# Attention scores of two heads in one product, with keys three units ahead, in a fused attention and feed-forward kernel

## The chip, the cores and the metric

The kernel runs on one core of one Trainium2 chip. The metric is device time in microseconds (us), from start to end of one execution; three executions of the kernel before stand below. The engines are TensorE (PE; its weight loads are listed apart as PEld), VectorE (DVE), ScalarE (ACT), GpSimd (POOL) and SyncE (SP), which issues every transfer of this kernel from one queue, in order.

## What is computed

Windowed attention with a few memory keys, then four gated feed-forward experts, then one more feed-forward layer with a leaky activation:

```python
for c in range(nc):                      # 24 chunks of 32 queries
    k_full = np.concatenate([mem_k, k_ctx], axis=2)   # 8 memory keys, 16 left, 32 own, 8 right
    v_full = np.concatenate([mem_v, v_ctx], axis=2)
    scores = scale * np.matmul(q_c, k_full.transpose(0, 1, 3, 2))
    scores = scores - np.max(scores, axis=-1, keepdims=True)
    a = np.exp(scores)
    a = a / (np.sum(a, axis=-1, keepdims=True) + 1e-09)
    out[:, :, c_start:c_end] = np.matmul(a, v_full)
...
for e in range(E):
    h = np.maximum(x @ w1[e], 0.0)
    out += p[:, e:e + 1] * (h @ w2[e])
...
h = x @ w_in
g = np.maximum(h, 0.0) + alpha * np.minimum(h, 0.0)
return g @ w_out
```

The batch is 2, with 8 heads, 768 positions and head size 64; the experts have 1024 hidden columns each, the last layer 2048. All is fp32.

## The kernel before

**Units.** Attention is cut into 12 units of 128 queries, taken in the order `TURN`. `unit(u)` is a generator that yields between its stages:

- scores on PE: `two<-qk`, 64 rows of the trace per unit. Heads stand in pairs, one head of a pair on partitions 0 to 63, the other on 64 to 127. Each product takes 64 partitions, 32 queries and the 64 keys of their window. The four windows of a block and the two heads of a pair use different parts of the array. The result lies in the two PSUM banks of `two`, one for each head of the pairs.
- the row maximum `mx` and the subtraction `pe` on DVE, then the exponential on ACT, in place in `pe`.
- four transposes `t` on PE, copied by ACT to `pt`.
- products with the values on PE: `x<-v,pt`, 32 rows of the trace per unit. Each takes all 128 partitions, both heads at once: the value tile holds zeros where one head's rows meet the other's columns. The first half of a unit's 32 rows reads value tile 2u, the second half tile 2u+1.
- the sums `dn` (ACT), the reciprocal `rd` and the scaling `xs` (DVE), four transposes `xt` (PE), and copies, sums and roundings into `acc`, `xh` and `xl`, from which the first expert's products read.

**Order.** For the first six units, `att_cycle` writes this order on PE: scores of unit m, value products of unit m-1, a few products on zeros (`keep_warm`, tile `keep`), transposes `t` of unit m and `xt` of unit m-1. From unit 6 on, products of the first expert (`a`, `b`, `d`, `c`) stand between the stages. Instructions issued through `Pinned` stay behind what was traced before them on their engine; the others (`nc.vector`, `nc.gpsimd`) are placed by the scheduler.

**Loads.** `load_qk(u)` brings queries and keys of one unit, 624 KB, in one transfer (unit 0 in two). `qk_all` holds two units. The load of unit u+2 is issued behind the scores of unit u, since it overwrites their keys. `load_v(hu)` brings the values of half a unit in two transfers of 64 partitions, 130 KB each, into one of five tiles `v0` to `v4`. A tile is loaded again when the value products have read it. At the start, DVE and POOL fill these tiles with zeros, and a tile's loads follow its two memsets. At the start SP issues unit 0, unit 1 and five value tiles, in this order.

**After attention.** From about 74 us to the end PE works through the experts and the last layer. Their weights are split on ACT, POOL and DVE; DVE adds the results to `acc`.

Of the kernel before, what the change touches and what calls it, by code (L numbers as in the profile page):

```python
# [10 lines left out]
F32 = mybir.dt.float32  # L11
# [7 lines left out]
B, H, S, D = 2, 8, 768, 64  # L19
CH, LEFT, RIGHT, MEM = 32, 16, 8, 8  # L20
BLK = 128
WIN = CH
NW = BLK // WIN
SHARE = LEFT + RIGHT
KEYS = MEM + LEFT + WIN + RIGHT
STEP = KEYS - SHARE
SPAN = NW * STEP + SHARE
NBLK = S // BLK
NU = B * NBLK
NT, DM = B * S, H * D  # L30
E, F1, F2 = 4, 1024, 2048
P = 128
KD = DM // P
HH = H // 2
HP = HH // 2
VW = 2 * HP * NW * (D + 1)
QW, KW = HP * BLK, HP * SPAN
# [26 lines left out]


@with_exitstack
def tile_kernel(ctx: ExitStack, tc: tile.TileContext, qk, v, wa, wq, dpt, alpha, out):
    nc = tc.nc
    scale = 1.0 / float(D) ** 0.5
    pe_, dve, act, pool, sync = (Pinned(tc, e) for e in (nc.tensor, nc.vector, nc.scalar, nc.gpsimd, nc.sync))  # L70
# [3 lines left out]
    bp = ctx.enter_context(tc.tile_pool(name="bp", bufs=1))  # L74
# [4 lines left out]
    two = scores.enter_context(tc.tile_pool(name="sc", bufs=1, space=bass.MemoryType.PSUM)).tile(  # L79
        [P, 2, 512], F32, tag="two", name="two")  # L80
# [36 lines left out]
    def fill(n):  # L117

        if n > 0:
            wps = alone(f"wps{now[0]}")  # L120
            for _ in range(n):
                pe_.matmul(wps[:, :2 * P].rearrange("p (a n) -> p a n", n=P), warm, warm.unsqueeze(1).to_broadcast([P, 2, P]),
                           start=True, stop=True)
                now[0] += 0.11

    fill(WARM)
    now[0] = 0.0
# [25 lines left out]
    xh = xp.tile([P, 14, NCOL], F32R, name="xh")  # L153
    xl = xp.tile([P, 14, NCOL], F32R, name="xl")

    half = NCOL // 2
    acc = xp.tile([P, KD, 2, 2, half], F32, name="acc")
# [5 lines left out]

    change = [False]
    spare = slice(NCOL // 2, NCOL)
    nc.gpsimd.memset(xh[:, 10:14, spare].bitcast(F32), 0.0)

    def keep_warm(u):

# [73 lines left out]
    def mm(*a, n, took=None, **kw):  # L243
        pe_.matmul(*a, **kw)
        now[0] += took or 0.013 + n / 2.4e3


    qk_all = bp.tile([P, RING, QW + KW], F32, tag="gg", bufs=2, name="qk")
# [3 lines left out]
    for vt in v_t:  # L252
        for e in range(2):
            (pool, dve)[e].memset(vt[:, e], 0.0)
    pt, xs, pe = (bp.tile([P, 2 * HP * BLK], F32, tag="ft", bufs=3, name=x) for x in ("pt", "xs", "pe"))
    pt = pt.rearrange("p (z q) -> p z q", q=BLK)
    xs = xs.rearrange("p (z e d) -> p z e d", e=2, d=D)
# [2 lines left out]
    def v_of(hu):  # L260
        return v_t[hu % RING_V]

    def load_qk(u, half=slice(0, 2)):
        if u >= NU:
            return
        i = 2 * u % RING
        sync.dma_start(qk_all[:, i + half.start:i + half.stop].rearrange("p h x -> p (h x)"),
                       qk[TURN[u], :, half].rearrange("p h x -> p (h x)"))

    v_next = [0]  # L270

    def load_v(hu):
        assert hu == v_next[0]
        v_next[0] += 1
        if hu >= 2 * NU:
            return
        for e in range(2):
            sync.dma_start(v_of(hu)[e::2, e].rearrange("p z w d -> p (z w d)"), v[TURN[hu // 2], e, :, hu % 2])

    def unit(u):  # L280
# [2 lines left out]
        cols = slice(c * BLK, (c + 1) * BLK)  # L283
        win = [slice(w * WIN, (w + 1) * WIN) for w in range(NW)]

        s_ps = two[:, :, :2 * HP * KEYS].rearrange("p e (z k) -> p e z k", k=KEYS)
        now[0] += T_SW
        for half in range(2):
            qk_ = qk_t[(2 * u + half) % RING]
            qv = qk_[:, :QW].rearrange("p (z q) -> p z q", q=BLK)  # L290
            kv = qk_[:, QW:].rearrange("p (z k) -> p z k", k=SPAN)
            for z in range(HP):
                for w in range(NW):
                    for e in range(2):
                        rows = slice(e * D, (e + 1) * D)
                        mm(s_ps[win[w], e, HP * half + z], qv[rows, z, win[w]], kv[rows, z, w * STEP:w * STEP + KEYS],
                           n=KEYS, took=T_S, start=True, stop=True)
        load_qk(u + RING // 2)
        mx = cp.tile([P, 2, 2 * HP], F32, tag="mx", bufs=2, name=f"mx{u}")
        dve.tensor_reduce(out=mx, in_=s_ps, axis=AX.X, op=ALU.max)  # L300
        dve.tensor_tensor(
            out=pe.rearrange("p z k e -> p e z k"), in0=s_ps,
# [17 lines left out]
        for z in range(2 * HP):  # L320
            half, i = divmod(z, HP)
            if z in CUT:
                n = CUT[z]
                parts.append((z, n, bank(f"x{u}_{z}")[:, :2 * n * (D + 1)].rearrange("p (z e d) -> p z e d", e=2, d=D + 1)))
            z0, _, x_ps = parts[-1]
            for w in range(NW):
                mm(x_ps[win[w], z - z0], pt[:, z, win[w]], v_of(2 * u + half)[:, :, i, w], n=2 * (D + 1), took=T_X,
                   start=True, stop=True)
            if i == HP - 1:
                load_v(2 * u + half + RING_V)  # L330
        dn = cp.tile([P, 2 * HP, 2, 1], F32, tag="dn", bufs=2, name=f"dn{u}")
# [48 lines left out]
        if c in MID:  # L380
# [4 lines left out]
            out=xl[:, 10:14, cols], in0=a2, in1=xh[:, 10:14, cols].bitcast(F32), op=sub)  # L385
# [10 lines left out]
    def att_poll(force=False):  # L396

        while True:
            due = [x for x in att["live"] if x[0] <= now[0] and clear(x[2])]
            room = att["next"] < NU and len(att["live"]) < LIVE and clear(att["next"])  # L400
            if due:
                x = due[0]
                try:
                    att["stage"][x[2]] += 1
                    lat = next(x[1])
                    x[0] = now[0] + lat
                except StopIteration:
                    att["live"].remove(x)
                    att["over"].add(x[2])
                    while att["done"] in att["over"]:  # L410
                        att["done"] += 1
            elif room and att["start"] <= now[0]:
                g = unit(att["next"])
                att["start"] = now[0] + (PACE0 if force else PACE)
                att["next"] += 1
                x = [0.0, g, att["next"] - 1]
                att["live"].append(x)
                x[0] = next(g) + now[0]
                att["stage"][x[2]] = 1
            elif force:  # L420
                times = [x[0] for x in att["live"] if clear(x[2])]
                if room:
                    times.append(att["start"])
                now[0] = max(now[0], min(times))
                continue
            else:
                return
# [3 lines left out]
    def att_cycle():  # L431
# [18 lines left out]
        def rest():  # L450
# [4 lines left out]
            begin()  # L455

        x = live[m] = [now[0], unit(m), m]
        att["live"].append(x)
        att["next"] += 1
# [139 lines left out]
    def weights():  # L599
        for p in range(NP):  # L600
            if p != NP1 + 1:
                yield from prep_w1(p)
            if p == NP1:
                yield from prep_w1(p + 1)
            yield from prep_w2(p)
# [61 lines left out]
    def stream(name, gen):  # L667
        streams[name] = [0.0, None, gen]
# [348 lines left out]
        order += [(1, k), (2, k - 1)]  # L1017
    order += [(2, len(tiles) - 1)]

    for i in range(2):  # L1020
        load_qk(0, slice(i, i + 1))
    load_qk(1)
    for hu in range(RING_V):
        load_v(hu)
    stream("w", weights())
    streams["w"][0] = PREP0
    acts = {}
# [26 lines left out]
    for i, (what, k, *other) in enumerate(order):  # L1054
        p, c0, n = tiles[k]
# [42 lines left out]
TURN = (0, 2, 1, 4, 3, 5, 6, 7, 8, 9, 10, 11)  # L1098
# [6 lines left out]
T_S, T_X, T_T, T_SW = 0.021, 0.06, 0.11, 0.1  # L1105
# [20 lines left out]
RING = 4  # L1126
V_ROOM = 1152
RING_V = 5
WARM = 18
PAD = 16  # L1130

# [72 lines left out]
```

## Time and profile before

| | us |
|---|---|
| runs of the kernel before | 808.28, 810.08, 810.2 |
| median | 810.08 |
| the profiled execution's own time | 810.12 |
| its span, first to last instruction | 808.3 |
| PE busy, share of the span | 795.1, 98% |
| DVE, ACT, POOL busy | 576.9, 324.8, 572.9 |
| granted TensorE clock | 1.000 |

The time outside the span (810.12 - 808.3 = 1.8 us) lies around the program. The page gives busy time, slices of the span, transfers, the chain of work that ended last, and groups of instructions. The views asked of the trace beside it are the chain in order of time, the timeline of an engine, and transfers issued in a stretch with their time to landing. Nearly every instruction has line 61, that of the helper `Pinned`, so rows are told apart by tile names. A line `x64` on PE counts rows of the trace: a product in plain fp32 that isn't a transpose shows as two of them, so the 32 score products that the program has for a unit are 64 rows.

### The profile page before, as it was taken

The numbers are of one execution on the slowest core, as the hardware profiler recorded it, in microseconds if no ns is written. First come the engines' busy times: TensorE is split into PE (matmuls) and PEld (weight loads), VectorE is DVE, ScalarE is ACT, GpSimd is POOL, SyncE is SP. The second block draws the span as 40 slices with busy tenths as digits, with TensorE's granted clock in tenths as the row PEclk, the third lists the DMA queues.
The fourth block names the chain that finished last, engine by engine and source line by source line (L and its number), as shares of the span: only waits on it lengthen the run. The fifth ranks groups of instructions, "written<-read, shape, count | busy, mean of one in ns | idle before, by whom it ended". The sixth has DMA issues, their size and how long they took to land.

```text
span 808.3 us, 13680 instructions
## 1 busy us (share of the span) xinstructions
PE 795.1 (98%) x5127; PEld 722.6 (89%) x5127; DVE 576.9 (71%) x1009; ACT 324.8 (40%) x726; POOL 572.9 (71%) x598
## 2 busy tenths in 40 slices
PE   7999999999999999999999999999999999999997
PEld 6779989989989889889899899999898988998996
DVE  4666367777777777777777878589975777676554
ACT  4667524224134133133133233154452664565441
POOL 2686767696796696696696783197764978978621
PEclk9999999999999999999999999999999999999999
DMA  8882111341331341322332312001002122221004
GB/s 250 275 276 78 53 53 40 118 143 40 118 103 42 118 124 60 118 78 66 118 106 79 106 51 89 4 27 50 30 26 92 51 81 89 81 92 66 1 1 156
DMA packets 29730, 71.62 MB, mean 89 GB/s; under 512 B 4448, under 2 KB 10592, under 8 KB 29664
## 3 DMA queue, kind: packets, MB, share of 16 engines
q1 hardware_dynamic: 29664, 70.75, 27.0%
q8 instruction: 40, 0.66, 0.3%
q14 instruction: 26, 0.21, 0.1%
HBM read 59.18 MB, written 11.56 MB: 88 GB/s over the span
## 4 chain that ended last, share of the span: by engine, by line
PE 90%; DVE 4%; POOL 2%; ACT 2%; issue 1%; DMA 1%; DVEq 0%; POOLq 0%; ACTq 0%
PE y L61 46%; PE d L61 12%; PE c L61 11%; PE a L61 11%; PE b L61 6%; PE two L61 1%; POOL gg L61 1%; DVE acc L61 1%; POOL xl L61 1%; PE x L61 1%; PE t L61 1%; DMA qk<-in_qk 1%; DVE pe L61 1%; DVE mx L61 1%; POOL wl L61 1%
## 5 line engine op out<-in xcount | busy, mean ns | idle before, releaser
L61 POOL TENSOR_TENSOR gg<-g,gg 128x384 fp32r<-128x384 f32 x192 | 206.7, 1088 | 111.7 <-ACT gg L61 111.2
L61 PE MATMUL y<-gg,wh 128*128 128x512 f32 (+1 forms) x816 | 244.6, 377 | 0.2 <-POOL gg L61 0.2
L61 DVE TENSOR_TENSOR acc<-y,acc 128x512 f32<-128x512 f32 (+1 forms) x244 | 162.4, 676 | 70.0 <-PE y L61 69.8
L61 PEld LDWEIGHTS y<-gg,wh 128*128 128x128 f32 x816 | 151.8, 188 | 24.8 <-POOL gg L61 0.6
L61 PE MATMUL y<-gg,wl 128*128 128x512 f32 (+1 forms) x408 | 153.8, 377 | 0.0
L61 ACT CAST gg<-g 128x384 fp32r<-128x384 f32 x192 | 95.9, 512 | 121.9 <-DVE g L61 121.1
L61 POOL TENSOR_TENSOR wl<-raw,wh 128x256 fp32r<-128x256 f32 (+1 forms) x110 | 111.7, 1020 | 29.4 <-ACT wh L61 27.4
L61 PE MATMUL y<-wh,gg 128*128 128x512 f32 x384 | 120.6, 390 | 0.0
L61 POOL TENSOR_TENSOR wl<-s,wh 128x256 fp32r<-128x256 f32 x88 | 67.0, 765 | 33.2 <-ACT wh L61 33.1
L61 PEld LDWEIGHTS y<-gg,wl 128*128 128x128 f32 x408 | 76.6, 188 | 12.1 <-issue 0.2
L61 PEld LDWEIGHTS y<-wh,gg 128*128 128x128 f32 x384 | 72.1, 188 | 14.7
L61 ACT COPY u<-a 128x384 f32<-128x384 f32 x48 | 23.0, 479 | 150.3 <-PE a L61 149.3
L61 PE MATMUL y<-wl,gg 128*128 128x512 f32 x192 | 74.9, 390 | 0.0
L61 PE MATMUL a<-xh,wh 128*128 128x384 f32 x184 | 62.0, 337 | 0.0
L61 PE MATMUL d<-xh,wh 128*128 128x384 f32 x184 | 61.8, 336 | 0.0
L61 PE MATMUL a<-xh,wl 128*128 128x384 f32 x184 | 61.8, 336 | 0.0
L61 PE MATMUL a<-xl,wh 128*128 128x384 f32 x184 | 61.6, 335 | 0.0
L61 PE MATMUL d<-xl,wh 128*128 128x384 f32 x184 | 61.6, 335 | 0.0
L61 PE MATMUL d<-xh,wl 128*128 128x384 f32 x184 | 61.6, 335 | 0.0
L61 DVE TENSOR_TENSOR u<-b,u 128x384 f32<-128x384 f32 x48 | 26.7, 555 | 48.3 <-PE b L61 48.0
L61 PE MATMUL c<-xl,wh 128*128 128x384 f32 x176 | 58.9, 335 | 0.0
L61 PE MATMUL c<-xh,wh 128*128 128x384 f32 x176 | 58.8, 334 | 0.0
(129 smaller groups left out, 1560.8 us busy)
## 6 DMA issues: line engine op xcount, KB each, us to landing
fr<-in_wq SPq DMA_DIRECT2D x32, 512.0 KB, 4.0
raw<-in_wa SPq DMA_DIRECT2D x28, 512.0 KB, 3.9
w2s<-fl SPq DMA_DIRECT2D x32, 256.0 KB, 2.4
raw<-w2s SPq DMA_DIRECT2D x16, 512.0 KB, 3.7
qk<-in_qk SPq DMA_DIRECT2D x11, 624.0 KB, 5.5
v<-in_v SPq DMA_DIRECT2D x48, 130.0 KB, 4.7
out<-acc SPq DMA_DIRECT2D x12, 256.0 KB, 2.4
pb<-p_dram SPq DMA_DIRECT2D x6, 384.0 KB, 3.8
```

The source lines that it names most:

```text
L61: return self.tc.keep_in_program_order(f(*a, **kw))
```

## The change

For the first six units (`WIDE_U`), scores of both heads of a pair come from one product over all 128 partitions. The keys lie among zeros: the first head's keys on partitions 0 to 63 of one column block and zeros below them, the second head's on partitions 64 to 127 of the next. A product takes 32 queries and 2 x 64 columns, and a unit has 16 in the program (32 rows of the trace) in place of 32 (64 rows). The result takes one bank of `two`, and units take turns.

These keys have three buffers (`WSLOTS`): two in a part of `acc` that is not yet in use, one in the new tile `wide`. The zeros are written once by `clear_k`, on POOL and DVE. A unit's load is now three transfers: queries (256 KB, 128 partitions) and the keys of either head (184 KB, 64 partitions each). The load of unit u+3 is issued behind the scores of unit u. Values follow the keys of their unit at the start (`FIRST_V`). The memset of `xh` that the `keep` products read is moved behind the value memsets on POOL. Units 6 to 11 are as before.

```diff
-    nc.gpsimd.memset(xh[:, 10:14, spare].bitcast(F32), 0.0)
+    wide = bp.tile([P, 2 * DM + 4 * KW], F32, tag="gg", bufs=2, name="wide")
+    def wide_k(u):
+        s = u % WSLOTS
+        x = acc[:, 2 * s:2 * s + 2, 1, :, :KW] if s < 2 else wide[:, 2 * DM:].rearrange("p (e h x) -> p e h x", e=2, h=2)
+        return x
+    def wide_q(u):
+        s = u % WSLOTS
+        return wide[:, s * DM:(s + 1) * DM] if s < 2 else qk_all[:, RING - 1, :DM]
+    def clear_k(u):
+        for e in range(2):
+            (nc.vector if e and u < 2 else nc.gpsimd).memset(wide_k(u)[e * D:(e + 1) * D, 1 - e], 0.0)
+    clear_k(0)
...
     for vt in v_t:
         for e in range(2):
             (pool, dve)[e].memset(vt[:, e], 0.0)
+    clear_k(1)
+    nc.gpsimd.memset(xh[:, 10:14, spare].bitcast(F32), 0.0)
+    for u in range(2, WSLOTS):
+        clear_k(u)
...
-    def load_qk(u, half=slice(0, 2)):
+    def load_qk(u):
...
+        if u < WIDE_U:
+            sync.dma_start(wide_q(u), qa[TURN[u]])
+            for e in range(2):
+                sync.dma_start(
+                    wide_k(u)[e * D:(e + 1) * D, e], ka[TURN[u], e * D:(e + 1) * D])
+            return
...
+        both = u < WIDE_U
+        if both:
+            s_ps = two[:, u % 2].rearrange("p (z e k) -> p e z k", e=2, k=KEYS)
+            qv = wide_q(u).rearrange("p (z q) -> p z q", q=BLK)
+            kv = wide_k(u).rearrange("p e h (z k) -> p h z e k", k=SPAN)
...
+        for z in range(2 * HP if both else 0):
+            for w in range(NW):
+                mm(s_ps[win[w], :, z], qv[:, z, win[w]], kv[:, z // HP, z % HP, :, w * STEP:w * STEP + KEYS],
+                   n=2 * KEYS, took=T_X, start=True, stop=True)
-        for half in range(2):
+        for half in range(0 if both else 2):
...
-        load_qk(u + RING // 2)
+        if u != WIDE_U - 2:
+            load_qk(u + (3 if u < WIDE_U - 2 else RING // 2))
+        for hu in FIRST_V[u + 3] if u + 3 < len(FIRST_V) else ():
+            load_v(hu)
...
-    for i in range(2):
-        load_qk(0, slice(i, i + 1))
-    load_qk(1)
-    for hu in range(RING_V):
-        load_v(hu)
+    for u in range(3):
+        load_qk(u)
+        for hu in FIRST_V[u]:
+            load_v(hu)
...
+FIRST_V = ((), (0, 1), (2, 3), (4,))
+WIDE_U = 6
+WSLOTS = 3
```

On PE, ACT and POOL the instructions keep their order, apart from the scores themselves and the memsets. Two places do move.

DVE at the start of the program, before. The names are value tiles `v0` to `v4`, and `mx0` and `pe`, the maximum and the subtraction of unit 0.

```order
L109 MEMSET tiny_83 128x1
L61 MEMSET v0_114 128x520
L61 MEMSET v1_115 128x520
L61 MEMSET v2_116 128x520
L61 MEMSET v3_117 128x520
L61 MEMSET v4_118 128x520
L61 TENSOR_REDUCE mx0_179<-two_75 128x8
L61 TENSOR_TENSOR pe_131<-two_75,mx0_179 128x2x256
L61 TENSOR_REDUCE mx1_236<-two_75 128x8
```

The same place in the changed kernel, where `acc` is the zeros among the keys:

```order
L180 MEMSET acc_111 64x2x368
L109 MEMSET tiny_83 128x1
L61 MEMSET v0_116 128x520
L180 MEMSET acc_111 64x2x368
L61 TENSOR_REDUCE mx0_178<-two_75 128x8
L61 TENSOR_TENSOR pe_138<-two_75,mx0_178 128x2x256
L61 MEMSET v1_117 128x520
L61 MEMSET v2_118 128x520
L61 MEMSET v3_119 128x520
L61 MEMSET v4_120 128x520
L61 TENSOR_REDUCE mx1_221<-two_75 128x8
```

The memsets of `v1` to `v4` moved behind the maximum and the subtraction of unit 0.

SP from the first value tile on, before:

```order
L61 DMA v0_114<-in_v 64x520 x2
L61 DMA v1_115<-in_v 64x520 x2
L61 DMA v2_116<-in_v 64x520 x2
L61 DMA v3_117<-in_v 64x520 x2
L61 DMA v4_118<-in_v 64x520 x2
L61 DMA qk_113<-in_qk 128x1248
L61 DMA raw0_0_183<-in_wa 128x256 x2
L61 DMA qk_113<-in_qk 128x1248
L61 DMA v0_114<-in_v 64x520 x2
L61 DMA v1_115<-in_v 64x520 x2
```

The same place in the changed kernel, as far as the second load of `v0`, which holds the values of half-unit 5. The transfers from `in_qa` and `in_ka` are a unit's queries and keys.

```order
L61 DMA v0_116<-in_v 64x520 x2
L61 DMA v1_117<-in_v 64x520 x2
L61 DMA qk_115<-in_qa 128x512
L61 DMA wide_112<-in_ka 64x736 x2
L61 DMA v2_118<-in_v 64x520 x2
L61 DMA v3_119<-in_v 64x520 x2
L61 DMA wide_112<-in_qa 128x512
L61 DMA acc_111<-in_ka 64x2x368 x2
L61 DMA v4_120<-in_v 64x520 x2
L61 DMA raw0_0_182<-in_wa 128x256 x2
L61 DMA wide_112<-in_qa 128x512
L61 DMA acc_111<-in_ka 64x2x368 x2
```

The loads of units 2, 3 and 4, three transfers each, now stand ahead of the second load of `v0`, which comes right behind these rows.

## Rows read from the trace of the kernel before

**Rows 1.** The page: busy time, and the chain that ended last by engine.

```profile
PE 795.1 (98%) x5127; PEld 722.6 (89%) x5127; DVE 576.9 (71%) x1009; ACT 324.8 (40%) x726; POOL 572.9 (71%) x598
...
PE 90%; DVE 4%; POOL 2%; ACT 2%; issue 1%; DMA 1%; DVEq 0%; POOLq 0%; ACTq 0%
```

**Rows 2.** The chain in order of time, 0 to 76 us: start, us, what.

```profile
9.50 5.21 DMA qk<-in_qk
...
19.39 1.49 issue
...
25.43 0.32 issue
...
42.49 0.21 issue
```

**Rows 3.** Timeline: start, us, engine, instructions, and the idle time before.

```profile
14.75 0.86 PE L61 MATMUL two<-qk 64*32 64x64 f32 x64 [1.49 <-DMA qk<-in_qk]
...
15.54 1.10 PE L61 MATMUL x<-v,pt 128*32 128x130 f32 x32
...
15.68 0.69 DVE L61 TENSOR_REDUCE mx<-two 128x8 f32<-128x512 f32 x1 [3.27 <-PE two L61]
```

**Rows 4.** Page, transfers: the queue that brings instructions.

```profile
q8 instruction: 40, 0.66, 0.3%
```

**Rows 5.** Timeline of PE: value products of units 2, 3, 4 and 5.

```profile
21.27 1.10 PE L61 MATMUL x<-v,pt 128*32 128x130 f32 x32
...
26.01 1.10 PE L61 MATMUL x<-v,pt 128*32 128x130 f32 x32
...
30.17 1.54 PE L61 MATMUL x<-v,pt 128*32 128x130 f32 x32
...
34.40 1.63 PE L61 MATMUL x<-v,pt 128*32 128x130 f32 x32
```

**Rows 6.** Timeline: the first unit on POOL, DVE and PE.

```profile
0.86 1.38 POOL L166 MEMSET xh<- 128x1536 f32 x1
...
1.12 2.69 DVE L61 MEMSET v<- 128x520 f32 x5
...
2.51 2.42 POOL L61 MEMSET v<- 128x520 f32 x5
...
4.92 1.18 PE L61 MATMUL two<-qk 64*32 64x64 f32 x64
...
6.15 0.69 DVE L61 TENSOR_REDUCE mx<-two 128x8 f32<-128x512 f32 x1 [2.34 <-PE two L61]
6.87 0.69 DVE L61 TENSOR_TENSOR pe<-two,mx 128x512 f32<-128x512 f32 x1
```

**Rows 7.** Timeline of SP: start, and time in which it issued.

```profile
0.73 1.35 SPq L61 DMA_DIRECT2D qk<-in_qk  x3
3.07 6.33 SPq L61 DMA_DIRECT2D v<-in_v  x10
9.50 1.60 SPq L61 DMA_DIRECT2D qk<-in_qk  x1
11.14 0.92 SPq L61 DMA_DIRECT2D raw<-in_wa  x2
...
15.08 0.59 SPq L61 DMA_DIRECT2D praw<-in_dpt  x1
```

**Rows 8.** Transfers issued at 54.4, 7.65, 20.0 and 12.6 us: count, KB, median us to landing.

```profile
v<-in_v SPq DMA_DIRECT2D x1, 130.0 KB, 2.8
...
v<-in_v SPq DMA_DIRECT2D x1, 130.0 KB, 3.2
...
v<-in_v SPq DMA_DIRECT2D x1, 130.0 KB, 4.5
...
v<-in_v SPq DMA_DIRECT2D x2, 130.0 KB, 6.1
```

**Rows 9.** Busy time by stretch: us, PE, PEld, DVE, ACT, POOL (instructions), granted clock, DMA share, GB/s.

```profile
9.00:15.00 6.00, 4.24 (x141) 3.38 (x142) 2.24 (x5) 2.77 (x6) 0.00 (x0) 1.00 0.75 210
```

More of the change, by code (lines that the diff above doesn't have):

```diff
@@ L66, in tile_kernel @@
 @with_exitstack
-def tile_kernel(ctx: ExitStack, tc: tile.TileContext, qk, v, wa, wq, dpt, alpha, out):
+def tile_kernel(ctx: ExitStack, tc: tile.TileContext, qa, ka, qk, v, wa, wq, dpt, alpha, out):
     nc = tc.nc
@@ L261, in v_of @@
         return v_t[hu % RING_V]
-    def load_qk(u, half=slice(0, 2)):
+    def load_qk(u):
         if u >= NU:
             return
+        if u < WIDE_U:
[4 more added lines that the diff above has]
+            return
         i = 2 * u % RING
-        sync.dma_start(qk_all[:, i + half.start:i + half.stop].rearrange("p h x -> p (h x)"),
-                       qk[TURN[u], :, half].rearrange("p h x -> p (h x)"))
+        sync.dma_start(qk_all[:, i:i + 2].rearrange("p h x -> p (h x)"), qk[TURN[u] - WIDE_U].rearrange("p h x -> p (h x)"))
     v_next = [0]
@@ L284, in unit @@
         win = [slice(w * WIN, (w + 1) * WIN) for w in range(NW)]
-        s_ps = two[:, :, :2 * HP * KEYS].rearrange("p e (z k) -> p e z k", k=KEYS)
-        now[0] += T_SW
-        for half in range(2):
+        both = u < WIDE_U
[3 more added lines that the diff above has]
+            kv = wide_k(u).rearrange("p e h (z k) -> p h z e k", k=SPAN)
+        else:
+            s_ps = two[:, :, :2 * HP * KEYS].rearrange("p e (z k) -> p e z k", k=KEYS)
+        now[0] += T_SW
+        for z in range(2 * HP if both else 0):
[3 more added lines that the diff above has]
+        for half in range(0 if both else 2):
             qk_ = qk_t[(2 * u + half) % RING]
@@ L1186 @@
     arrays = {
-        "qk": qk,
+        "qa": np.ascontiguousarray(qk[:WIDE_U, :, :, :QW]).reshape(WIDE_U, P, 2 * QW),
+        "ka": np.ascontiguousarray(qk[:WIDE_U, :, :, QW:]),
+        "qk": np.ascontiguousarray(qk[WIDE_U:]),
         "v": np.ascontiguousarray(vs).reshape(NU, 2, KEYS, 2, HP * NW * (D + 1)),
```

## The prediction

> **What bounds the kernel now.** The page comes first. PE is busy 98% of the span and holds 90% of the chain that ended last [rows 1]. From about 74 us to the end PE hardly pauses and the change touches nothing there, so the only question is how much earlier or later PE gets through the first six units, at about 5 to 40 us.
>
> The chain in order of time is read next, for the losses there. It waits for the keys of unit 2, and then it shows "issue" three times [rows 2]. The timeline prices the first: PE stood still 1.49 us before unit 2's scores at 14.75 [rows 3]. The "issue" pauses of 1.49, 0.32 and 0.21 us come when no tile is late. Instructions arrive in 40 packets of 0.66 MB in all, some 16 KB each [rows 4], and a paused PE waiting for the next packet fits. The value products show the same: 32 rows take 1.10 us, but 1.54 in unit 4 and 1.63 in unit 5 [rows 5], 0.44 and 0.53 more. These pauses add up to 1.49 + 0.32 + 0.44 + 0.53 + 0.21 = 3.0 us.
>
> The third view is SP's timeline. At the start one value transfer follows the other every 0.64 us (9.50 - 3.07, over ten), and a load of queries and keys takes 0.45 (1.35 over three) [rows 7]. SP is a queue with a price per transfer, and the change adds transfers to it.
>
> **The change, part by part.**
>
> *Scores, slower by 0.24 us a unit.* The new products have the shape of the value products, 128 partitions by 32 and 128 columns against 130, and 32 rows of the trace. Those take 1.10 us [rows 3, 5]; the 64 old rows take 0.86 [rows 3]. Fewer instructions, yet 0.24 us more. The maximum waits for all of them, so this lies on the path in each unit. Below, the old 0.86 halved would be 0.43; I take 1.10, since shape and row count match. Unit 0 loses nothing: there the old scores took 1.18 [rows 6].
>
> *Fewer PE instructions.* A unit issues 32 rows fewer of weight loads and as many of products, 64 x 6 = 384 instructions. PE and PEld have 2 x 5127 rows [rows 1], 256 for each of the 40 packets, so that is one packet and a half. PE reaches the next packet later, so I count the four pauses up to unit 5 as gone and the 0.21 too, and give 0.3 us back for pauses at new places (bounds 0 and 1.5, the largest one seen).
>
> *The wait for unit 2's keys* goes: they are issued before unit 1's scores have ended, not at 9.50.
>
> *The memset of `xh`* moves behind the value memsets on POOL, with two key memsets before it. By size, 0.9 ns an element [rows 6], it ends near 0.9 + 0.7 + 0.3 + 2.4 + 0.7 + 1.4 = 6.4 us, and the first `keep` products need it. Those and the transposes behind them stay at about their old place: the exponential ends then anyway. Cost 0.
>
> *SP, first step: a new wait.* The order rows show the memsets of `v1` to `v4` on DVE behind unit 0's maximum and subtraction. Only each other, not the maximum, holds them in place. A tile's load follows its memset, so SP, which issues in order, stands still at `v1` until DVE has done the maximum (6.15), the subtraction (6.87, 0.69 us) and one memset of 2.69 / 5 = 0.54 us [rows 6]: 8.15 us. Before, the second value tile went out at about 4.4. Everything behind it on SP waits too, unit 2's keys among it.
>
> *SP, second step: three transfers for one.* Up to the second transfer of half-unit 5 SP then issues nine value transfers at 0.64, three of queries at 0.45, six of keys, and two of `raw` at 0.5 (0.92 us for two, and the gap) [rows 7]. The price of a key transfer isn't in the trace. It has 64 partitions as the values do (0.64) and rows of 1472 or 2944 bytes; queries and keys of 128 partitions take 0.45. I take 0.55, between the two. The sum is 5.8 + 1.35 + 3.3 + 1.0 = 11.4, so half-unit 5's last transfer is issued at 8.15 + 11.4 = 19.6 us. A value transfer lands 2.8 us later at best, 3.2 when issued with little ahead of it, 4.5 and 6.1 when the queue is full [rows 8]. SP is now the slow side, so I take 3.2: 22.8. Unit 2's second half of value products began at 21.27 + 0.55 = 21.8 [rows 5]. It begins **1.0 us later**, though its scores are done earlier.
>
> *Then half-unit 7.* Behind it on SP come one value transfer at 0.64, two more, one of 0.59 for `praw`, two of `raw`, unit 5's load (0.45 + 1.1) and one value transfer: 0.64 + 1.3 + 0.6 + 1.0 + 1.55 + 0.64 = 5.7. Issued at 25.3, landed at 28.5. Unit 3's second half began at 26.01 + 0.55 = 26.6 [rows 5]: **1.9 us later**. PE is there first: it finishes unit 2 near 23.4 and needs some 4 us to this place.
>
> *After that* SP keeps up. Two transfers of half-unit 8, unit 6's load, now a single transfer, and two of half-unit 9 take 3.0 us, so half-unit 9 lands near 31.5, and unit 4's second half is due near 33. Nothing waits for values again.
>
> *The sum.* +1.9 at unit 3's value products; +0.24 for unit 5's scores (those of unit 4 hide behind the wait for half-unit 7); -0.44, -0.53 and -0.21 for pauses that go; +0.3 for new ones. That is +1.3 us. The pauses of 1.49 and 0.32 and the wait for unit 2's keys, 3.3 us together, are won before unit 3's value products and spent waiting for them. Against the profiled execution's own 810.12 us this gives 811.4; that execution lies at the median of the runs (810.08).
>
> The Trainium skill (DMA: Bandwidth & Descriptors, Rules for kernel authors) speaks against this load: two transfers to disjoint halves of the partitions serialize, and one of 128 partitions should be used. By that rule the two key transfers buy nothing for their two places in the queue; with one, 0.45 in place of 1.1 us a unit, half-unit 7 would be issued 4 x 0.65 = 2.6 us earlier, and the sum would be -1.3.
>
> **The rivals.**
>
> *The values land later still: slower.* Place: the last transfer of half-unit 7. Price: 4.5 us to landing in place of 3.2 [rows 8] adds 1.3, and a key transfer at the values' 0.64 adds 0.09 for each of eight, 0.7. Together +3.3, 813.4; at 6.1 us it would be 815. It decides from 1.1 us over my sum. For it: most value transfers before took over 4 us. Against: those stood behind 624 KB in one piece, and SP now feeds the queue slowly. Chance 0.33.
>
> *PE stands still long enough to lose its clock: slower.* In unit 2 it would wait from about 20.5 to 22.8, longer than any pause before, where the granted clock stays at 1.00 through a pause of 1.49 [rows 3, 9], the 2.4 GHz level. At 1.2 GHz the next scores and value products would take 1.10 us more each, some 2.5 us over a unit: 814. The Trainium skill (TensorE: Matmul & The Clock Gate, Part 1) says that an idle TensorE falls back to 1.2 GHz; no run here shows it. Chance 0.07.
>
> *SP isn't late: faster.* If key transfers take 0.4 and values land in 2.5 us, half-unit 7 arrives at 26.6. PE, which would have its 3.3 less 0.24 for each of units 1 to 3, asks for it near 24.0: it still waits, comes out even there, and the sum is -0.6, 809.5. Only with scores at 0.43 and DVE's memsets early would all of 3.3 + 1.2 be kept: 806. Chance of over 0.3% faster 0.07.
>
> *The change doesn't do what it says*: keys three units ahead but no gain from it, since values set the pace. That is the forecast itself.
>
> **How the numbers follow.** A measurement of this kernel can tell about 0.3%, 2.4 us, from no change. My forecast, +1.3, lies inside, with chance 0.53 for the cases within 2.4 us (key transfers from 0.40 to 0.64, landing from 2.5 to 4). The two slower rivals have 0.40, the faster one 0.07. The range for 8 in 10 leaves out a tenth at either end: from 809.0 (the even case, less half a microsecond for unpriced gains) to 814.5 (landing at 4.5 with the dear key transfer, and a part of the lost clock).
>
> **What would show it.** Right: DVE's memsets of `v1` to `v4` begin near 7.6; SP issues nothing from about 5.5 to 8.1; scores of 16 products take about 1.1 us; no wait for keys at unit 2; PE waits for the values in the middle of `x` of units 2 and 3, until about 22.8 and 28.5. Wrong: value products of units 2 and 3 without a pause, or "issue" pauses as long as before, or a granted clock below 1.00. If the key transfers show 0.4 us in SP's row, the sum falls by a microsecond; if units 6 to 11 wait for anything new, it is too low.

## The result, and the profile after

The changed kernel takes 816.27 us (median; 815.71 to 816.91 in four runs) against 809.59 before: a ratio of 1.0085, 95% interval 1.0072 to 1.0097. It is slower by some 6.7 us; 811.4 with a range of 809.0 to 814.5 had been forecast. The profiled execution took 816.55 us.

The page of the kernel after: busy time, the instruction queue, and the chain that ended last [rows 1, 4].

```profile
PE 798.7 (98%) x4935; PEld 726.4 (89%) x4935; DVE 579.0 (71%) x1011; ACT 324.8 (40%) x726; POOL 575.8 (71%) x602
...
q8 instruction: 39, 0.64, 0.3%
...
PE 90%; DVE 3%; POOL 2%; DMA 2%; ACT 1%; issue 1%; SPq 0%; DVEq 0%; ACTq 0%; POOLq 0%
```

PE issues 192 products fewer, and DMA has gone from 1% to 2% of the chain. The timeline after, first of PE, then of DVE, then of SP (start, us in which it worked or issued, and in brackets the idle time before and what ended it) [rows 3, 5 to 7]:

```profile
5.72 1.94 PE L61 MATMUL two<-acc,wide 128*32 128x128 f32 x32 [0.72 <-DMA acc<-in_ka]
7.58 2.76 PE L61 MATMUL keep<-xh 128*128 128x384 f32 x10
...
16.43 1.08 PE L61 MATMUL two<-wide,qk 128*32 128x128 f32 x32 [0.73 <-DMA wide<-in_ka]
...
22.52 0.65 PE L61 MATMUL x<-v,pt 128*32 128x130 f32 x16
27.97 1.09 PE L61 MATMUL x<-v,pt 128*32 128x130 f32 x16 [4.79 <-DMA v<-in_v]
28.99 1.97 PE L61 MATMUL keep<-xh 128*128 128x384 f32 x5
...
32.59 1.32 PE L61 MATMUL two<-acc,wide 128*32 128x128 f32 x32
...
38.10 1.07 PE L61 MATMUL x<-v,pt 128*32 128x130 f32 x32
...
7.71 0.69 DVE L61 TENSOR_REDUCE mx<-two 128x8 f32<-128x512 f32 x1 [4.33 <-PE two L61]
8.44 0.69 DVE L61 TENSOR_TENSOR pe<-two,mx 128x512 f32<-128x512 f32 x1
9.19 2.14 DVE L61 MEMSET v<- 128x520 f32 x4
...
1.18 1.32 SPq L61 DMA_DIRECT2D acc<-in_ka  x2
...
4.48 6.37 SPq L61 DMA_DIRECT2D v<-in_v  x4
10.89 0.58 SPq L61 DMA_DIRECT2D qk<-in_qa  x1
11.52 2.25 SPq L61 DMA_DIRECT2D wide<-in_ka  x2
13.88 2.45 SPq L61 DMA_DIRECT2D v<-in_v  x4
...
22.43 3.21 SPq L61 DMA_DIRECT2D v<-in_v  x4
```

SP's waits up to 40 us, the first line of that view (us in total, times, longest):

```profile
SPq L61 <- DVE v L61: 4.0, 1, 4.0
```

The chain in order of time, at the loss:

```profile
23.02 4.81 DMA v<-in_v
...
27.97 1.09 PE x L61 x16
```

Busy time by stretch, with the granted clock before the last two columns:

```profile
20.00:25.00 5.00, 2.48 (x57) 2.00 (x55) 1.77 (x4) 2.13 (x5) 2.06 (x3) 1.00 0.87 240
25.00:30.00 5.00, 2.03 (x19) 1.67 (x20) 0.49 (x2) 1.15 (x4) 1.49 (x5) 0.63 0.90 183
```

Read from the top. Unit 0's scores start at 5.72, where they had started at 4.92 [rows 6], and they and `keep` take long, 1.94 us for what takes 1.08 in unit 2: that is the pace of the lower of PE's two clock levels, 1.2 GHz. (The level is read from these rows; the trace's record of the clock begins at 9.24 us, and the views show 1.00 before that.) Unit 0's maximum comes at 7.71 in place of 6.15. Behind it and the subtraction stand DVE's memsets, behind those `v1` to `v4`, and SP waits 4.0 us within its four value transfers from 4.48. From then on SP issues one transfer after the other. The last transfer of half-unit 5 goes out at 23.02 and lands 4.81 us later, and PE stands 4.79 us in the middle of unit 2's value products. There it loses its clock, granted 0.50 from 28 to 33 us: `keep` takes 1.97 us for 1.16. Unit 4's scores begin at 32.59, where they had begun at 24.69: 7.9 us late. Some of that comes back, since the pauses without a tile are gone (`x` of unit 4 takes 1.07 us for 1.54 [rows 5]), and the end is 6.4 us later in the profiled executions.

### The profile page after: what moved, and what is told of

Read it like the earlier page. It is cut to its first block, busy times and chain, and to the rows that moved or that the text cites. A ratio compares the mean times of both kernels' runs of the same rounds, so it can differ in the third digit from the quotient of the medians.

```text
span 814.7 us, 13323 instructions
## 1 busy us (share of the span) xinstructions
PE 798.7 (98%) x4935; PEld 726.4 (89%) x4935; DVE 579.0 (71%) x1011; ACT 324.8 (40%) x726; POOL 575.8 (71%) x602
## 4 chain that ended last, share of the span: by engine, by line
PE 90%; DVE 3%; POOL 2%; DMA 2%; ACT 1%; issue 1%; SPq 0%; DVEq 0%; ACTq 0%; POOLq 0%
PE y L61 47%; PE d L61 12%; PE c L61 11%; PE a L61 11%; PE b L61 6%; PE two L61 1%; DMA acc<-in_ka 1%; DMA v<-in_v 1%; POOL gg L61 1%; POOL xl L61 1%; DVE pe L61 1%; DVE mx L61 1%; POOL wl L61 1%; PE x L61 1%; SPq L61 0%
```

## Experiments

Four theories stand in the first expectation. Each median is followed by the ratio to the kernel before, run on the same chip.

**1. DVE's memsets ahead of unit 0's maximum**

```diff
-            (nc.vector if e and u < 2 else nc.gpsimd).memset(wide_k(u)...
+            ((dve if u else nc.vector) if e and u < 2 else nc.gpsimd).memset(wide_k(u)...
```

> The changed kernel with one edit: the memset of unit 1's keys on DVE is issued in program order, so that the memsets of v1 to v4 go ahead of unit 0's maximum and subtraction. Four theories on the 6.7 us that were lost. T1 (DVE's order holds SP): v1's transfers go out near 5.7 instead of 9.7, the last transfer of half-unit 5 near 19.0 instead of 23.0, the 4.79 us wait in unit 2's value products falls below 1 us, and the time is 809.5 to 812. T2 (the nine small transfers of each unit fill SP and the queue): SP goes on sooner but the queue is full instead; the wait stays above 2.5 us and the time at 814 or more. T3 (the clock lost in that wait): the granted clock at 26 to 33 us stays at 1.00 if the wait falls below 1.5 us, and the time falls by the wait and some 1.8 us more. T4 (values queued behind the keys of later units): wait of 2 to 4 us, 812.5 to 814.

813.51 us, ratio 1.0053 (1.0038 to 1.0068). PE's timeline:

```profile
23.76 0.65 PE L61 MATMUL x<-v,pt 128*32 128x130 f32 x16 [2.92 <-DMA v<-in_v]
24.34 1.16 PE L61 MATMUL keep<-xh 128*128 128x384 f32 x5
...
30.15 0.65 PE L61 MATMUL x<-v,pt 128*32 128x130 f32 x16 [2.30 <-DMA v<-in_v]
```

The hold is gone and 2.8 us come back, less than half of the loss. There are two waits now, at unit 2 and at unit 3, at full clock. SP issues half-unit 5 near T1's time (19.35 us for 19.0), but the wait is 2.92 us where T1 had under 1, and the time is not T1's either. The chain in order of time shows what both waits consist of, the landing of half-units 5 and 7:

```profile
19.35 4.27 DMA v<-in_v
...
25.78 4.24 DMA v<-in_v
```

T1 is part of the cause.

**2. The DVE hold alone, in the kernel before**

```diff
-        for e in range(2):
+        for e in range(2 if i == 0 else 1):
             (pool, dve)[e].memset(vt[:, e], 0.0)
...
+        if u == 0:
+            for vt in v_t[1:]:
+                dve.memset(vt[:, 1], 0.0)
+            for hu in range(1, RING_V):
+                load_v(hu)
+            load_qk(2)
```

> The kernel before with one part of the change alone: the DVE memsets of v1 to v4 behind unit 0's subtraction, and the loads of v1 to v4 and of unit 2's keys behind those memsets; single transfers of queries and keys and the old scores stay. T1: a late start of the value loads costs by itself: 811.5 to 813, waits for values in units 1 and 2. T2 and T4: single transfers leave SP room to catch up, the time is within 1 us of before (809 to 810.5).

813.88 us, 1.0052 (1.0037 to 1.0067): 4.3 us, more than T1 said. PE waits 1.59 us for values in unit 0, then for the keys of unit 2, and is at the lower clock after that:

```profile
17.20 1.06 PE L61 MATMUL two<-qk 64*32 64x64 f32 x64 [3.48 <-DMA qk<-in_qk]
18.19 1.96 PE L61 MATMUL x<-v,pt 128*32 128x130 f32 x32
```

A late start of SP isn't made up, although every load here is a single transfer.

**3. The cut of the loads alone, in the kernel before**

```diff
+        if u < 6:
+            sync.dma_start(slot(u)[:, :2 * QW], qk[TURN[u], :, :2 * QW])
+            for e in range(2):
+                rows = slice(e * D, (e + 1) * D)
+                sync.dma_start(slot(u)[rows, 2 * QW:], qk[TURN[u], rows, 2 * QW:])
+            return
```

> The kernel before with the transfer count of the change alone: queries and keys of units 0 to 5 come as three transfers each (queries of 128 partitions, keys twice 64 partitions), at the old places; memsets, scores and two buffers as before. T1: SP has room, 809.5 to 811. T2: two more places of 0.6 us a unit on SP and smaller transfers in the queue; waits for keys or values appear in units 1 to 5, 812 to 815.

813.81 us, 1.0055 (1.0039 to 1.0070), as T2 said. PE waits for each half of the keys in turn (the profiled execution, 815.59 us, is the slowest of the six; 2.6 us of it are two stops after 52 us, later than the units with cut loads):

```profile
15.87 0.27 PE L61 MATMUL two<-qk 64*32 64x64 f32 x2 [1.86 <-DMA qk<-in_qk]
17.32 0.84 PE L61 MATMUL two<-qk 64*32 64x64 f32 x62 [1.18 <-DMA qk<-in_qk]
```

**4. The prefetch alone, in the kernel before**

```diff
+    def slot(u):
+        s = u % 3 if u < 6 else u % 2
+        return third if s == 2 else qk_all[:, 2 * s:2 * s + 2]
...
-        load_qk(u + RING // 2)
+        if u != 5:
+            load_qk(u + (3 if u < 5 else 2))
```

> The kernel before with the prefetch of the change alone: three buffers for queries and keys of units 0 to 5 (the third in the second gg buffer), each load three units ahead as single transfer, unit 2's behind v0 and v1; memsets and scores as before. The prefetch is what was to win the time: the 1.49 us stop before unit 2's scores goes or shrinks, 808.3 to 809.3 by T1 and T2 (0.3 to 1.3 us faster than before). T4 (values behind the keys of later units): values of units 1 and 2 land later by a transfer each, 810 to 811.

809.66 us, 1.0005 (0.9993 to 1.0017): no difference. The chain in order of time:

```profile
13.15 0.88 PE two L61 x53
...
17.77 2.11 issue
19.87 0.68 PE two L61 x31
20.55 1.89 PE x L61 x32
```

Unit 2's scores begin 1.7 us earlier, as wanted. Then PE stands 2.11 us in the middle of unit 3's scores, waiting for no tile, where it had stood 1.49 us in the same scores [rows 2], and it loses its clock on top (granted 0.50 from 20 to 25 us). So in this execution, at 810.95 us slower than the median, the expected gain is real up to unit 2 and is given back one unit later.

**5. Values ahead of the later keys** (on the kernel of run 1)

```diff
-        if u != WIDE_U - 2:
-            load_qk(u + (3 if u < WIDE_U - 2 else RING // 2))
+        if u >= WIDE_U - 1:
+            load_qk(u + RING // 2)
...
                 load_v(2 * u + half + RING_V)
+        if u < WIDE_U - 2:
+            load_qk(u + 3)
```

> The changed kernel with the pinned DVE memset of the first experiment, and the load of queries and keys of units 3 to 5 issued behind the value loads of the unit three before, in place of ahead of them. T4 (values stand behind keys that are needed later): half-unit 5 goes out some 2 us earlier, the waits of 2.92 and 2.30 us in the value products of units 2 and 3 fall below 1 us each, and the time goes from 813.5 to 809.5 to 811. T2 (the number of small transfers is what SP and the queue can't carry): what the values win the keys lose; PE waits for keys of units 3 and 4 instead, 812.5 to 814.

814.35 us, 1.0065 (1.0044 to 1.0086). T4 falls: no value product waits any more, and the keys are late instead.

```profile
21.92 1.14 PE L61 MATMUL two<-acc,wide 128*32 128x128 f32 x32 [3.59 <-DMA acc<-in_ka]
...
28.83 1.08 PE L61 MATMUL two<-acc,wide 128*32 128x128 f32 x32 [1.42 <-DMA acc<-in_ka]
```

**6. PE kept at work in the wait** (on the changed kernel)

```diff
+            if u == 2 and z == HP:
+                o = alone("wait2")[:, :2 * P].rearrange("p (a n) -> p a n", n=P)
+                for _ in range(36):
+                    pe_.matmul(o, warm, warm.unsqueeze(1).to_broadcast([P, 2, P]), start=True, stop=True)
```

> The changed kernel, and in the middle of unit 2's value products 36 products of zeros, which nothing reads, so that PE works through most of the 4.79 us wait for half-unit 5. T3 (the wait also takes PE's clock): the granted clock stays at 1.00 from 26 to 33 us, the rows behind the wait take what they take elsewhere (value products of half a unit 0.65 us for 1.09, keep 1.16 for 1.97, transposes 0.63 for 1.05), and the time falls by 1.5 to 2 us, to 814.3 to 814.8. If the clock is no part of it: 816 to 817.

818.16 us, 1.0103 (1.0086 to 1.0120): no faster than the change itself (1.0085; the intervals overlap). The clock is held where it had been lost, and the time goes into the next wait, where the clock falls instead:

```profile
28.60 1.15 PE L61 MATMUL keep<-xh 128*128 128x384 f32 x5
...
34.23 0.65 PE L61 MATMUL x<-v,pt 128*32 128x130 f32 x16 [2.12 <-DMA v<-in_v]
34.81 1.75 PE L61 MATMUL keep<-xh 128*128 128x384 f32 x5
```

T3 was right on the rows and wrong on the time: PE goes at the pace of the values (the second half of unit 2's value products starts at 28.02 us, at 27.97 in the changed kernel), and holding its clock in this wait wins nothing.

**7. Keys of units 0 to 2 issued by ScalarE** (on run 1): `(act if u < 3 else sync).dma_start(wide_k(u)...`

> The changed kernel with the pinned DVE memset of the first experiment, and the six key transfers of units 0 to 2 issued by ScalarE, which is idle then, in place of SP; the same bytes in the same pieces. T2 by SP's places: SP is 3.7 us further on with everything behind unit 0, unit 0's scores start at 5.0 in place of 5.5, half-unit 5 lands 2 to 3 us earlier and the waits in units 2 and 3 go: 809.5 to 811. T2 by the transfers themselves (the DMA engines are busy 0.97 of the time from 5 to 15 us at 255 to 268 GB/s): the same transfers wait in the queue in place of on SP, latencies over 6 us, 812.5 to 814.

812.81 us, 1.0034 (1.0022 to 1.0046), some 0.7 less than run 1, whose interval overlaps. Up to 15 us SP now waits 4.8 us for transfers issued before to land, 0.2 in run 1, and unit 0's scores start at 6.03, later. The wait in unit 2 falls to 1.27 us and that in unit 3 grows to 2.97. Inconclusive between the two forms of T2.

**8. More products at the start** (on the changed kernel): `WARM = 22` for 18.

> The changed kernel with 22 in place of 18 products of zeros at the start, so that PE works until unit 0's keys land and doesn't pause 0.72 us there. T3 at the start: the clock rises 2 to 3 us earlier, unit 0's scores take 1.1 to 1.3 us in place of 1.94 and the products behind them 2.0 in place of 2.76; with unit 0's maximum DVE's memsets and SP come 1 to 1.5 us earlier too, and the time is 814.5 to 815.5. If the late clock has another cause than the pause: 816 to 817.

816.78 us, 1.0085 (1.0071 to 1.0099): no change. Unit 0's scores take 1.08 us and `keep` 2.04, so the clock did rise earlier, although PE still paused 1.28 us. That the four products did it is not shown: run 6, with 18, has 1.08 and 2.02 us at the same place after a pause of 1.33, so this differs from one execution to the next. The gain is spent at once, in a wait of 1.86 us for `v1` (2.22 in run 6).

**9. First raw and praw transfers issued by ScalarE** (on run 1): `act.dma_start` for `sync.dma_start` at these five.

> The changed kernel with the pinned DVE memset of the first experiment, and the first four raw transfers and the praw transfer issued by ScalarE in place of SP: five places fewer on SP ahead of half-unit 7, the same transfers in the queue. T2 by SP's places (five of 0.44 to 1.15 us, some 3 us): half-unit 5 lands 1 us earlier and half-unit 7 2.5 to 3 us earlier, the waits of 2.92 and 2.30 us fall to some 2 and under 0.5 us, 810.5 to 812. T2 by bytes and pieces in the DMA engines: no change in the landings, 813 to 814.

813.29 us, 1.0051 (1.0036 to 1.0067): no gain. Unit 3's wait is gone, but unit 2's is 3.33 us and takes the clock with it. The transfers were issued earlier than on SP (9.4 us for 15.1), into the values' way, and SP waits 1.2 us for them to land, so the run moved more than SP's places; a miss.

**10. Eleven transfers of 16 bytes a row, in the kernel before**

```diff
+        load_qk_(u, half)
+        if u < 6 and half.stop == 2:
+            for i in range(1 if u == 0 else 2):
+                sync.dma_start(bits[i * D:(i + 1) * D, 2 * u + i], qk[u, i * D:(i + 1) * D, 0, :4])
```

> The kernel before, and behind the loads of queries and keys of units 0 to 5 eleven more transfers of 64 partitions by 16 bytes into a tile that nothing reads: the transfer count of the change on SP without its bytes moved or cut differently. T2 by SP's places: eleven times 0.5 to 0.6 us on SP ahead of unit 5's end; keys and values of units 1 to 5 come 1 to 4 us later, as where the loads were split, 812 to 814.5. T2 by the cut of the loads (64-partition pieces are slow in the engines): 809.5 to 811.

812.84 us, 1.0042 (1.0030 to 1.0055). Eleven KB in all cost 3.8 us, about what the cut of the loads costs. SP's timeline and PE's:

```profile
2.89 1.16 SPq L61 DMA_DIRECT2D bits<-in_qk  x2
4.16 7.29 SPq L61 DMA_DIRECT2D v<-in_v  x10
11.55 0.53 SPq L61 DMA_DIRECT2D qk<-in_qk  x1
...
15.73 1.18 PE L61 MATMUL two<-qk 64*32 64x64 f32 x64 [2.80 <-DMA qk<-in_qk]
```

Unit 2's keys go out at 11.55 for 9.50 [rows 7]. As that issue took 1.60 us before and takes 0.53 here, it ends 1.0 us later, and the scores begin 1.0 us later, 15.73 for 14.75 [rows 3]. Behind the longer wait PE is at the lower clock (granted 0.50 from 15 to 20 us), so a part of the 3.8 us is the clock's. What sets it off is T2 by SP's places, since hardly a byte was added.

**11. Keys of units 1 to 5 issued by ScalarE, and 12. the raw and praw transfers too** (on run 1)

```diff
+    def load_k(u):
+        for e in range(2):
+            (act if u else sync).dma_start(wide_k(u)[e * D:(e + 1) * D, e], ka[TURN[u], e * D:(e + 1) * D])
...
         act.copy(pt, t_ps)
+        if u + 3 < WIDE_U:
+            load_k(u + 3)
```

> The changed kernel with the pinned DVE memset of the first experiment, and the key transfers of units 1 to 5 issued by ScalarE, those of units 3 to 5 behind the copy of the transposed weights of the unit three before; unit 0's stay on SP. Ten places of 0.6 us leave SP. T2 by SP's places: no wait over 1 us for values in units 2 and 3, 808.5 to 811. T2 by bytes and pieces: 812.5 to 814.

> The two together: key transfers of units 1 to 5 and the first raw and praw transfers issued by ScalarE, pinned DVE memset. SP then issues only queries and values at the start. T2 by SP's places: PE waits for nothing in units 2 to 5, and the 1.7 us that the prefetch alone won up to unit 2 appear, 807.5 to 809.5, faster than before. T2 by bytes and pieces: 812 to 814; ScalarE now issues 15 transfers of some 0.6 us, of which up to 2 us may come to lie on the path.

813.03 us, 1.0049 (1.0037 to 1.0061), and 815.53 us, 1.0086 (1.0069 to 1.0104). The first line of SP's waits in each:

```profile
SPq L61 <- DMA acc<-in_ka: 4.4, 4, 2.4
```

```profile
SPq L61 <- DMA acc<-in_ka: 5.9, 4, 2.6
```

The places leave SP and the time doesn't follow. Of run 11's 4.4 us SP waits 2.9 for its own transfers of unit 0's keys, which land at 6.6 and 8.2 us beside ScalarE's four key transfers (4.7 and 5.4 in run 1), and 1.5 for ScalarE's; unit 0's scores start 2 to 3 us later (8.38 and 7.50). A place costs its 0.6 us on ScalarE too, and ScalarE waits as SP does: in run 12 two key transfers take it 2.68 us, and behind them PE waits 2.21 us for an exponential.

```profile
23.83 2.68 ACTq L61 DMA_DIRECT2D wide<-in_ka  x2
```

These waits come from the program: its transfers report their landing on eight semaphores in turn, and one is used again only when the transfer before has landed. In the changed kernel this holds SP for 0.2 us up to 40 us, so it isn't what made that kernel slow. That neither repair worked doesn't refute SP's places; moving them cost what it saved.

**13. No key transfers for units 3 to 5, and 14. the same transfers with 16 bytes** (on run 1)

```diff
-            for e in range(2):
+            for e in range(2 if u < 3 else 0):
```

```diff
+            h, n = (slice(0, 2), KW) if u < 3 else (slice(0, 1 if u == 5 else 2), 4)
             for e in range(2):
-                    wide_k(u)[e * D:(e + 1) * D, e], ka[TURN[u], e * D:(e + 1) * D])
+                    wide_k(u)[e * D:(e + 1) * D, e, h, :n], ka[TURN[u], e * D:(e + 1) * D, h, :n])
```

> The changed kernel with the pinned DVE memset of the first experiment, and the six key transfers of units 3 to 5 left out (those units score against the keys that lie in the buffers). What the rest would do if these keys cost nothing. T2 in either form: the waits of 2.92 and 2.30 us in the value products of units 2 and 3 go, unit 6's scores start near 33.5 for 37.1, and the time is 808 to 810.5. If something else than the key loads holds units 2 to 5 (the start, the wider products, the order): 812 to 814.

> The same, but the six key transfers of units 3 to 5 stay in their places on SP and move 16 bytes a row and head in place of 1472 (those units score against the keys that lie in the buffers): places without bytes. T2 by SP's places: hardly better than with whole keys, 812 to 813.5, waits of 1.5 us or more left. T2 by bytes in the engines: as with the transfers left out, 808 to 810.5. Between the two if both carry it.

809.40 us, 1.0003 (0.9989 to 1.0018; single runs from 807.3 to 814.0), without the six transfers; 812.93 us, 1.0042 (1.0029 to 1.0055), with them almost empty; 813.51 us whole, in run 1. So by the medians six places on SP cost 3.5 us, clear of the noise, and the 1.1 MB that they carry 0.6, which is not (the intervals of runs 1 and 14 overlap). By stretch, run 14:

```profile
15.00:20.00 5.00, 4.31 (x88) 3.34 (x77) 2.80 (x6) 3.40 (x8) 2.07 (x3) 1.00 0.66 175
20.00:25.00 5.00, 2.79 (x23) 2.48 (x24) 1.65 (x4) 1.53 (x4) 1.61 (x6) 0.77 0.59 133
```

and its PE, with nearly the wait of run 1 (2.92 us) in unit 2:

```profile
22.21 0.69 PE L61 MATMUL x<-v,pt 128*32 128x130 f32 x16 [2.59 <-DMA v<-in_v]
```

The DMA engines are busy only 0.59 to 0.66 of these stretches, the last but one column. The transfer that PE waits for there, half-unit 5's last, goes out at 16.14 us in run 13, at 18.84 in run 14 and at 19.35 in run 1, and lands at 19.76, 22.07 and 23.62. So four empty places ahead of it cost 2.3 us at the landing, and their bytes some 1.5 more. After that, run 14's chain in order of time is SP itself up to half-unit 7's last transfer, where run 1's was the landing:

```profile
19.66 1.18 SPq L61
...
24.88 0.54 SPq L61
...
25.46 2.87 DMA v<-in_v
```

For the keys of units 3 to 5 the places are the larger part of T2, and the bytes a smaller one. Two things stay unsettled. Behind its wait in unit 2 run 14 loses PE's clock (granted 0.77 from 20 to 25 us), which run 1's profile doesn't show, so the 3.5 us are not SP's time alone. And the keys of units 0 to 2 weren't emptied: in run 1 the engines are busy 0.98 and 0.97 from 5 to 10 and 10 to 15 us, where bytes may count for more. No version here beats the kernel before: the prefetch alone is even with it.

## Why the prediction was wrong, step by step

- *Scores, +0.24 us a unit*: right, 1.08 us for 0.86.
- *PE's pauses*: right. Value products take 1.07 and 1.10 us in units 4 and 5. But nothing was won by it before unit 4, since PE was waiting for values by then.
- *The wait for unit 2's keys goes*: wrong. They stand behind the stopped values on SP, go out at 10.89 to 13.77, and scores wait 0.73 us for them, to 16.43, later than before (14.75).
- *`xh` memset at nothing*: right, `keep` starts right behind unit 0's scores.
- *SP stands still at `v1`*: the mechanism is right and shown by run 1, which gives 2.8 us back, and by run 2. It was sized at 8.15 us and ended at 9.74: unit 0's keys come in two late pieces, PE starts them 0.8 us later and at the lower clock, and the maximum, on which the memsets hang, is 1.6 us later (7.71 for 6.15; in run 6's profile, with unit 0 at full clock, it is still 1.1 us later). That unit 0 would start on time was never put in question; the step lacked this term.
- *Twenty SP transfers in 11.4 us*: they took 13.3, from 9.74 to 23.02. Key transfers took 0.6 us (1.21 for two at 17.00) against the 0.55 taken, one of them 1.72 (below), and SP waited 0.7 us for PE to free what it was to load into.
- *Landing 3.2 us after issue*: 4.81.

The last three, the hold, SP's pace and the landing, are the step that failed: half-unit 5's last transfer was put at 19.6 + 3.2 = 22.8 and landed at 27.83. Of these 5.0 us, 1.6 are the hold, 1.8 or 1.9 SP's pace and 1.6 the landing. "1.0 us later" for unit 2's second half became 6.15. The wait at half-unit 7, put at 1.9 us, was then covered by it and never showed. Run 1 shows the landing by itself: without the hold SP issues the last transfers of half-units 5 and 7 at 19.35 and 25.78 us, close to the 19.6 and 25.3 of the forecast, but they land 4.27 and 4.24 us later in place of 3.2, and the time is 813.51 us, still 2.1 over the forecast. The 3.2 was read from a transfer with little ahead of it, and the 4.5 that the rival used was the nearer row.

The rival *values land later still* named the mechanism with a chance of 0.33, but put its place at half-unit 7 and its price at 3.3 us; it was at half-unit 5 and twice as dear. *PE loses its clock* had 0.07 and happened, with `x`, `keep` and the transposes at nearly double time from 27.97 to 32.6; run 6 shows that holding it in this wait wins nothing. *The change doesn't do what it says*, "since values set the pace", was the better sentence for the changed kernel. In run 4 keys in time win nothing either, but there the gain is lost in a stop without a tile, not to values.

The rule that the prediction weighed (the Trainium skill, DMA: Bandwidth & Descriptors, Rules for kernel authors: one transfer of 128 partitions in place of two to disjoint halves) agrees with run 3, where the cut of one load into three costs 4.2 us by itself. Its reason, that both halves share the same DMA engines, seems the smaller part here: run 10 pays 3.8 us for transfers with hardly a byte. The same page of the Trainium skill (Issuing engines are not separate DMA queues) says that issuing from several engines saves only issue time, usually small beside the transfer. Here the places that issue takes were most of the price by runs 13, 14 and 1, 3.5 of 4.1 us, and runs 11 and 12 show no gain from moving them to ScalarE (813.03 and 815.53 us against run 1's 813.51).

What stays open: how the 6.7 us divide exactly. The parts alone (4.3 for the hold, 4.2 for the cut) add up to more than the whole, as one wait can cover another. How much of the start's 1.8 us (unit 1's scores begin at 10.71 for 8.93) would have stayed, and what the bytes of units 0 to 2 cost, was not isolated.

## What to carry to other kernels

A queue that issues one transfer after the other is an engine with a price per instruction: count its places between two due times, at the dearest price that the trace shows for such a transfer and not at the mean, before counting bytes, and take the landing from a stretch with as many transfers in flight (4.3 to 4.8 us here, where 3.2 was taken). When all work in a stretch hangs on such a queue, cutting one load into three for the sake of another engine's products can cost more than they are worth (4.2 us here, by itself); and a prefetch that puts places ahead of what is due first delays it. A wait that is put ahead of the whole queue (a memset behind a maximum) delays all that stands behind it: without SP's wait of 4.0 us the changed kernel is 2.8 us faster (run 1), and such a hold, put alone into the kernel before, cost 4.3 (run 2).

## What the runs showed of the hardware

SP's long pauses go with the fetch of instructions: all five SP transfers of the kernel after that took over 1 us to issue before 70 us (1.3 to 1.7 us in the first two) overlap the fetch of a packet of instructions, and end some 0.2 to 0.4 us behind it. The transfers view from 12 to 14 us, over SP's 1.72 us at 12.05:

```profile
q8 instruction: 1, 0.02, 4.2%
```

The kernel before shows the same in all its five (one, of 2.37 us, over three packets). Not every packet costs SP that: over the one fetched at 36.05 us in the kernel after, transfers take 0.60 and 0.70 us to issue; and run 4 has one long issue, 1.26 us at 13.58, without a packet. PE's stop of 1.49 us at 19.39 in the kernel before [rows 2] begins within a packet, too, fetched from 18.54 to 19.52 us; that it waits for it is argued, not shown. The pause was not in the forecast, and the one at 12.05 is 1.1 us of SP's 13.3.

A pause's length didn't decide whether the clock fell: it stayed at full through the 2.92 and 2.30 us waits of run 1 (granted 1.00 from 20 to 35 us) and fell in the 2.11 us stop of run 4 (granted 0.50 from 20 to 25).
